# Key transposes evacuated in 1024-column tiles by one engine, and output products of 512 columns with a fold

## The chip, the cores and the metric

The kernel runs on one core of one Trainium2 chip. The time is device microseconds of one execution. Its engines are TensorE (PE, with its weight loads shown as PEld), VectorE (DVE), ScalarE (ACT), GpSimd (POOL) and SyncE (SP); 16 DMA engines move data between HBM and the on-chip memory SBUF. TensorE writes into PSUM, eight banks of 512 float32 columns in each of 128 partitions. Only DVE and ACT read PSUM here.

## The reference

One decoding step for two rows x of 512 numbers. Everything is float32.

```
xn  = layernorm(x)
q   = xn @ wq                                  # 32 heads of 128
k,v = the last 4096 positions of the caches    # 8 key/value heads, each serves 4 query heads
o   = softmax(q . k / sqrt(128)) @ v           # per head
A   = o @ wo                                   # 4096 -> 512
h   = relu(xn @ W_gate) * (xn @ W_up)          # 512 -> 1792
B   = h @ W_down                               # 1792 -> 512
out = x + A + B
```

The keys and values are 2 x 8 x 4096 x 128 numbers each, 67 MB together. The weights are another 28 MB.

## The kernel before

All large inputs go through one ring of four SBUF buffers (`ring`, 32 KB a partition each), in program order, by DMAs that SP issues. A load waits on SP until the buffer of the load four places ahead of it is released. The order is wq in two parts, W_gate, W_up, then key and value tiles of 4 MB, then W_down, then wo in two parts of 4 MB (the second cut into rows 0 to 7, 8 to 12, 13 to 14 and 15).

The attention is done in four groups g (batch row and half of the key/value heads), each with two key tiles and two value tiles (a = 0, 1; two heads each). The order of instructions is written out by hand: the tile framework is told to keep it and only adds the waits. Each engine runs its own instructions strictly in that order.

A key tile arrives as 64 blocks of 128 x 128 (positions by head dimension) and has to be transposed. `transposes` (L308 to L319) does it in two halves (s1 = 0, 1) of 32 blocks: four blocks go into one PSUM tile `pk` of 512 columns, and `evacuate` (L304 to L306) copies it to the SBUF tile `kT`, the copies taken in turn by ACT and DVE. `pk` has three buffers in the pool `ps_kt`, whose tag `kt` also serves `q_ps`, `qt`, `g_ps`, `u_ps`, `pp` and `y_ps`. `scores` (L322) multiplies a finished half of `kT` with the queries, 16 instructions of 512 columns in four column groups of 32. It runs one half behind the transposes.

`softmax(g - 1)` (L335) is a generator. Its steps are put between the transposes of key tile (g, 0), from the third PSUM tile on, by `kwork` (L432): the row maximum `m` and its transpose `mt` and combination `mx`, `mb` on DVE, the bias `nm` by a small matmul, the exponentials `p` on ACT, then two transposed halves `pp` in PSUM, which DVE multiplies with a mask into `pt`.

`values` (L386) multiplies `pt` with a value tile, 32 instructions of 512 columns in four column groups, and `evacuate` copies the sum `o` to `on`. `gather` (L404) picks each head's rows with four matmuls of 128 columns; `finish` (L414) scales by the softmax's sum. `spread_heads` (L420) brings the heads of two groups into the transposed form `oT` that the last product needs.

The last product: `project` (L478) adds one row block (128 inputs) to `y_ps`, as four matmuls of 128 columns in four column groups. It is called for the 17 blocks of W_down, then for the 2 x 16 blocks of wo, as their loads land. `y_ps` is copied to `yo` and stored.

Before the groups, the kernel computes xn, the queries, and the hidden layer `hh`, `hx`, whose transposes `ht_ps` (104 + 8 small matmuls) become `hT`.

Of the kernel before, what the change touches and what calls it, by code (L numbers as in the profile page):

```python
# [20 lines left out]
def kernel(  # L21
# [12 lines left out]
    nc = tc.nc  # L34
    P = 128
    B, _, D = x.shape
    _, HKV, SK, DH = k_cache.shape
# [86 lines left out]
    NJ = HQ * DH // (R * P)  # L124
    NE = DH // NJ
    HR = HQ // R
# [11 lines left out]
    ident = const.tile([P, P], F32, name="ident")  # L138
# [5 lines left out]
    ones = const.tile([1, 1], F32, name="ones")  # L144
# [6 lines left out]
    hx = const.tile([32, SX, 64], F32, name="hx")  # L151
# [19 lines left out]
    )  # L171


    HK = 2 * REP
    by_h = const.tile([P, NP, HK], F32, name="by_h")
    nc.vector.tensor_reduce(
# [66 lines left out]

    g_ps = ps_kt.tile([P, MQ], F32, name="g_ps", tag="kt")
    u_ps = ps_kt.tile([P, MQ], F32, name="u_ps", tag="kt")
    x_ps = ps_1.tile([32, 2, FX], F32, name="x_ps", tag="o0")
    for h, dst, wt in ((0, g_ps, gw), (1, u_ps, uw)):
        for kc in range(KC):
            for c in range(Q):
# [28 lines left out]
    for i in range(LEFT):  # L278
# [1 line left out]
        nc.vector.tensor_tensor(  # L280
            hx[:, RX, i:32:4], gx[:, 1, lo:lo + 8], x_ps[:, 1, lo:lo + 8], op=ALU.mult
        )
    ht_ps = ps_1.tile([P, FM + SX, B], F32, name="ht_ps", tag="misc")
    for k in range(FM):
        for c in range(Q):
            nc.tensor.matmul(
                ht_ps[32 * c:32 * c + 32, k], hh[:, k], ident[:, 32 * c:32 * c + B], start=True, stop=True
            )
    for k in range(SX):
        m = 64 if k < RX else 32  # L290
        nc.tensor.matmul(ht_ps[0:m, FM + k], hx[:, k, 0:m], ident[0:32, 0:B], start=True, stop=True)
    nc.vector.tensor_copy(hT[:, 0:FM, :, 0], ht_ps[:, 0:FM])
    nc.vector.tensor_copy(hT[0:64, FM:FM + RX, :, 0], ht_ps[0:64, FM:FM + RX])
    if LEFT:
        nc.vector.tensor_copy(hT[0:32, FM + RX, :, 0], ht_ps[0:32, FM + RX])

    HW = W // S1
    ss, pts, rls = {}, {}, {}  # L300
    kts, osb = {}, {}
    turn = [0]

    def evacuate(dst, src):  # L304
        (nc.vector.tensor_copy if turn[0] % 2 else nc.scalar.copy)(dst, src)  # L305
        turn[0] += 1  # L306

    def transposes(g, a, s1, kt_in):  # L308

        kt = ktp.tile([P, 2, HW], F32, name=f"kT{g}_{a}_{s1}", tag="kT")  # L310
        kts[g, a, s1] = kt
        for n in range(2 * Q):
            pk = ps_kt.tile([P, 512], F32, name=f"pk{g}_{a}_{s1}_{n}", tag="kt")
            for u in range(4):
                j = 8 * Q * s1 + 4 * n + u
                nc.tensor.transpose(pk[:, u * P:(u + 1) * P], kt_in[:, j * P:(j + 1) * P], ident)  # L316
# [18 lines left out]
    def softmax(g):  # L335

        m = work.tile([P, 1], F32, name=f"m{g}", tag="m")
        nc.vector.tensor_reduce(out=m, in_=ss[g], op=ALU.max, axis=AX.X)
# [8 lines left out]
        nc.vector.tensor_scalar(  # L347
            mb, mx[:, :, None, :].to_broadcast([1, NP, S1, HK]), -SCALE, None, op0=ALU.mult
        )
        yield  # L350
        nm_ps = ps_1.tile([P, 1], F32, name=f"nm_ps{g}", tag="misc")
        for q in range(Q):
            nc.tensor.matmul(
                nm_ps[32 * q:32 * q + 32, :], mb.rearrange("p a s k -> p (a s k)"), ones, start=True, stop=True
            )
# [12 lines left out]
        pv = p.rearrange("r y h -> r (y h)")  # L368
        for jh in range(2):
            pp = ps_kt.tile([P, 4, P], F32, name=f"pp{g}_{jh}", tag="kt")  # L370
            for u in range(4):
                lo = (4 * jh + u) * P
                nc.tensor.transpose(pp[:, u], pv[:, lo:lo + P], ident)  # L373
            nc.vector.tensor_tensor(  # L374
                pts[g][:, jh].rearrange("p n u k -> p u n k"), pp.rearrange("p u (n k) -> p u n k", k=HK),
                own.rearrange("p h i -> p (h i)")[:, None, None, :].to_broadcast([P, 4, Q * NP * S1, HK]), op=ALU.mult,
            )
# [6 lines left out]
    ons = {}  # L384

    def values(g, a, v):  # L386
        o = ps_1.tile([P, 512], F32, name=f"o{g}_{a}", tag=f"o{a}")
        for s1 in range(S1):
            for jh in range(2):
                for q in range(Q):  # L390
                    n = (q * NP + a) * S1 + s1
                    lo = (8 * Q * s1 + 8 * q + 4 * jh) * P
                    nc.tensor.matmul(  # L393
                        o[32 * q:32 * q + 32, :],
                        pts[g][:, jh, n].rearrange("p u k -> p (u k)"), v[:, lo:lo + 512],
                        start=(s1 == 0 and jh == 0), stop=(s1 == S1 - 1 and jh == 1),
                    )
# [6 lines left out]
    def gather(g, a):  # L404

        if a == 0:
            oa[g] = ps_1.tile([HR, P], F32, name=f"oa{g}", tag="oa")
        for u in range(4):
            nc.tensor.matmul(  # L409
                oa[g], pick[:, u, 8 - 8 * a:24 - 8 * a], ons[a][:, u],  # L410
                start=(a == 0 and u == 0), stop=(a == NP - 1 and u == 3),
            )

    def finish(g):  # L414
        r, b = divmod(g, B)
        if b == 0:
            osb[r] = const.tile([HR, B, P], F32, name=f"osb{r}")
        nc.vector.tensor_scalar(osb[r][:, b], oa[g], rls[g], 2.0, op0=ALU.mult, op1=ALU.mult)

    def spread_heads(r):  # L420
        op = ps_1.tile([P, NJ, B], F32, name=f"op{r}", tag="misc")
# [53 lines left out]
            x2[:, e * P:(e + 1) * P], start=True, stop=False,  # L475
        )

    def project(lhsT, w, stop):  # L478
        for e in range(Q):
            nc.tensor.matmul(  # L480
                y_ps[32 * e:32 * e + 17, :], lhsT.rearrange("p b s -> p (b s)")[:, 0:17],
                w[:, e * P:(e + 1) * P], start=False, stop=stop,
            )

    for a in range(NP):
# [1 line left out]
        gather(g, a)  # L487
    finish(g)
    for k in range(FM):
        project(hT[:, k], dw[:, k], False)  # L490
    for k in range(SX):
        n = 64 if k < RX else 32
        project(hT[0:n, FM + k], wx[0:n, k], False)
    spread_heads(R - 1)
    for r, cuts in ((0, (0, NJ)), (1, (0, 8, 13, 15, NJ))):
        wt = ring.tile([P, NJ, D], F32, name=f"wo{r}", tag="ring")
        for j0, j1 in zip(cuts, cuts[1:]):
# [34 lines left out]
```

## Time and profile before

| | |
|---|---|
| median of 3 runs | 231.21 us (231.04 to 231.34) |
| the profiled execution's own time | 231.43 us |
| its span, first to last instruction | 229.6 us |
| mean granted TensorE clock | 0.938 |
| moved by DMA | 95.15 MB, 414 GB/s on average |
| busy: PE, DVE, ACT | 81%, 29%, 20% of the span |

The span is what the trace covers; the profiled execution's own time has 1.8 us around it. In the rows shown below, a line is: kernel line, engine, operation, output <- inputs, shapes, then either the group's busy time and the mean nanoseconds of one, or (in the timeline) start and duration in microseconds, with the idle time before and what ended it in brackets. A float32 matmul is two PE instructions, a transpose one. Ends of matmuls are modelled, so starts are the safer numbers on PE.

### The profile page before, as it was taken

The page shows a single profiled execution, that of the slowest core. Times are in us where ns is not written, and L with a number is a line of the kernel's source. Part 1 is how long each engine was busy: PE and PEld are TensorE (multiplying, and loading weights), DVE is VectorE, ACT ScalarE, POOL GpSimd, SP SyncE. Part 2 cuts the span into 40 slices and gives each one's busy share as a digit, 9 for nine tenths or more (in the row PEclk, how much of TensorE's full clock was granted, in tenths as well). Part 3 has the DMA queues.
Part 4 walks back from the last instruction along what each step waited for, and adds up shares of the span by engine and source line. Part 5 has one row for each costly group of instructions (what it writes and reads, how often), then busy time and mean ns, then how long its engine had stood idle before and what let it go on. Part 6 is the DMA issues. An engine that isn't in the chain of part 4 may idle for free.

```text
span 229.6 us, 4149 instructions
## 1 busy us (share of the span) xinstructions
PE 185.4 (81%) x1876; PEld 114.7 (50%) x1876; DVE 67.2 (29%) x135; ACT 46.9 (20%) x80; POOL 8.2 (4%) x25
## 2 busy tenths in 40 slices
PE   0059961779999899997799699889979973988794
PEld 0052231259666583663484566458446532247682
DVE  0320021034444570441472143157124224001000
ACT  0020100004344451440351233045023202010000
POOL 8100000000000000000000000000000300000000
PEclk9999999577999999999999799999999999599678
DMA  7999999999999999999999999999999999999981
GB/s 274 451 428 408 454 410 437 422 451 442 405 425 451 415 417 445 442 411 420 457 417 432 428 440 414 434 445 414 422 440 437 417 428 440 423 442 414 410 364 49
DMA packets 3824, 95.15 MB, mean 414 GB/s; under 512 B 434, under 2 KB 448, under 8 KB 704
## 3 DMA queue, kind: packets, MB, share of 16 engines
q1 hardware_dynamic: 3796, 94.90, 96.7%
q8 instruction: 14, 0.23, 0.4%
q14 instruction: 2, 0.02, 0.0%
q10 hardware_dynamic: 12, 0.00, 0.0%
HBM read 94.90 MB, written 0.00 MB: 413 GB/s over the span
## 4 chain that ended last, share of the span: by engine, by line
DMA 54%; PE 41%; DVE 2%; issue 1%; ACT 1%; ACTq 0%; POOL 0%; DVEq 0%
DMA k<-in_A_k_cache_dram 37%; PE pk L316 21%; DMA wo<-in_A_wo_dram 13%; PE s L329 7%; PE y_ps L480 5%; DMA x<-in_A_x_dram 4%; PE o L393 3%; PE q_ps L222 3%; PE xt_ps L212 2%; ACT p L362 1%; PE pp L373 0%; ACTq L135 0%; PE oa L409 0%; DVE stats L189 0%; DVE kT L305 0%
## 5 line engine op out<-in xcount | busy, mean ns | idle before, releaser
L316 PE MATMUL pk<-ident,k 128*128 128x128 f32 x512 | 67.9, 286 | 6.0 <-DMA k<-in_A_k_cache_dram 5.9
L316 PEld LDWEIGHTS pk<-ident,k 128*128 128x128 f32 x512 | 57.9, 146 | 20.9 <-issue 16.7
L305 DVE COPY kT<-pk 128x512 f32<-128x512 f32 x64 | 44.2, 691 | 52.1 <-PE pk L316 46.2
L305 ACT COPY kT<-pk 128x512 f32<-128x512 f32 x64 | 37.5, 585 | 69.5 <-PE pk L316 69.5
L393 PE MATMUL o<-v,pt 128*32 128x512 f32 x256 | 32.5, 641 | 0.0
L329 PE MATMUL s<-kT,qz 128*32 128x512 f32 x256 | 30.9, 598 | 0.0
L393 PEld LDWEIGHTS o<-v,pt 128*32 128x32 f32 x256 | 11.3, 117 | 15.7 <-issue 10.9
L212 PE MATMUL xt_ps<-rep,xn 2*128 2x32 f32 x16 | 3.7, 400 | 13.9 <-DVE xn L206 13.9
L329 PEld LDWEIGHTS s<-kT,qz 128*32 128x32 f32 x256 | 7.1, 109 | 11.9 <-issue 11.5
L305 DVE COPY on<-o 128x512 f32<-128x512 f32 x4 | 2.8, 692 | 30.5 <-PE o L393 30.5
L409 PE MATMUL oa<-on,pick 128*16 128x128 f32 x64 | 8.3, 273 | 4.1 <-DVE on L305 3.3
L480 PE MATMUL y_ps<-wo,oT 128*17 128x128 f32 x256 | 10.3, 329 | 1.6 <-DMA wo<-in_A_wo_dram 1.6
L409 PEld LDWEIGHTS oa<-on,pick 128*16 128x16 f32 x64 | 5.8, 97 | 11.3 <-DVE on L305 7.0
L250 PE MATMUL u_ps<-wu,xnT 128*32 128x416 f32 x32 | 5.8, 901 | 6.1 <-DMA wu<-in_B_W_up_dram 6.1
L212 PEld LDWEIGHTS xt_ps<-rep,xn 2*128 2x128 f32 x16 | 3.6, 320 | 13.9 <-issue 13.9
L222 PE MATMUL q_ps<-wq,xnT 128*32 128x512 f32 x64 | 9.7, 777 | 0.5 <-DVE xnT L214 0.5
L480 PEld LDWEIGHTS y_ps<-wo,oT 128*17 128x17 f32 x256 | 8.1, 119 | 3.6 <-DMA wo<-in_A_wo_dram 2.6
L305 ACT COPY on<-o 128x512 f32<-128x512 f32 x4 | 2.3, 586 | 27.0 <-PE o L393 27.0
L98 POOL MEMSET wx<- 64x2048 f32 x1 | 1.8, 1804 | 169.1 <-PE s L329 169.1
L362 ACT ACTIVATE p<-s,nm 128x1024 f32<-128x1024 f32 x4 | 4.5, 1114 | 13.1 <-DVE nm L357 13.1
L374 DVE TENSOR_TENSOR pt<-pp,own 128x512 f32<-128x512 f32 x8 | 5.4, 689 | 2.6 <-PE pp L373 2.6
L373 PE MATMUL pp<-ident,p 128*128 128x128 f32 x32 | 4.9, 280 | 1.7 <-ACT p L362 1.5
(83 smaller groups left out, 68.2 us busy)
## 6 DMA issues: line engine op xcount, KB each, us to landing
k<-in_A_k_cache_dram SPq DMA_DIRECT2D x8, 4096.0 KB, 23.9
v<-in_A_v_cache_dram SPq DMA_DIRECT2D x8, 4096.0 KB, 28.3
wq<-in_A_wq_dram SPq DMA_DIRECT2D x2, 4096.0 KB, 21.7
wo<-in_A_wo_dram SPq DMA_DIRECT2D x1, 4096.0 KB
wg<-in_B_W_gate_dram SPq DMA_DIRECT2D x1, 3584.0 KB, 29.8
wu<-in_B_W_up_dram SPq DMA_DIRECT2D x1, 3584.0 KB, 39.3
wd<-in_B_W_down_dram SPq DMA_DIRECT2D x1, 3328.0 KB
wo<-in_A_wo_dram SPq DMA_DIRECT2D x1, 2048.0 KB
```

The lines of the kernel that those rows point to most:

```text
L212: nc.tensor.matmul(xt_ps[:, o, kc, :], cols, rep.rearrange("r s b -> r (s b)"), start=True, stop=True)
L222: nc.tensor.matmul(q_ps[r][32 * c:32 * c + 32, :], xnT[:, 0, kc, :], wqt[kc // 2][:, kc % 2, n * 512:(n + 1) * 512], start=(kc == 0), stop ...
L250: nc.tensor.matmul(dst[32 * c:32 * c + 32, :], xnT[:, 1, kc, :], wt[:, kc, c * MQ:(c + 1) * MQ], start=(kc == 0), stop=(kc == KC - 1),)
L305: (nc.vector.tensor_copy if turn[0] % 2 else nc.scalar.copy)(dst, src)
L316: nc.tensor.transpose(pk[:, u * P:(u + 1) * P], kt_in[:, j * P:(j + 1) * P], ident)
L329: nc.tensor.matmul(ss[g][32 * q:32 * q + 32, :], qz[:, g, 32 * n:32 * n + 32], kt[:, h, q * 512:(q + 1) * 512], start=(a == 0 and s1 == 0 ...
L362: nc.scalar.activation(p, both, AF.Exp, bias=nm, scale=SCALE, accum_out=l)
L373: nc.tensor.transpose(pp[:, u], pv[:, lo:lo + P], ident)
L374: nc.vector.tensor_tensor(pts[g][:, jh].rearrange("p n u k -> p u n k"), pp.rearrange("p u (n k) -> p u n k", k=HK), own.rearrange("p h i ...
L393: nc.tensor.matmul(o[32 * q:32 * q + 32, :], pts[g][:, jh, n].rearrange("p u k -> p (u k)"), v[:, lo:lo + 512], start=(s1 == 0 and jh == 0 ...
L409: nc.tensor.matmul(oa[g], pick[:, u, 8 - 8 * a:24 - 8 * a], ons[a][:, u], start=(a == 0 and u == 0), stop=(a == NP - 1 and u == 3),)
L480: nc.tensor.matmul(y_ps[32 * e:32 * e + 17, :], lhsT.rearrange("p b s -> p (b s)")[:, 0:17], w[:, e * P:(e + 1) * P], start=False, stop=stop,)
```

## The change

The transposes of a half go into four PSUM tiles of 1024 columns (two banks), eight blocks each, with two buffers instead of three; DVE copies all of them, ACT none. The generator still yields eight times a half: after four blocks and after the copy. `o` has one buffer instead of two. `on` is no longer a copy but a product with a row mask on DVE; `gather` is then one matmul of 512 columns, and `finish` adds up its four parts with one DVE reduction. `mb` is written four times wide by two DVE instructions, and `nm` comes from one matmul instead of four. `ht_ps` is made by 13 + 4 matmuls with a strided identity, and copied by five DVE copies. Three constants are added.

In the last product, `slot` multiplies one row block by all 512 columns in one matmul; four blocks in turn use the four column groups of a second PSUM tile `y4`. That serves W_down, the first half of wo and rows 0 to 7 of the second half. Then DVE copies `y4` to `ys`, four matmuls with the constant `fold` add its column groups into `y_ps`, and the last eight rows of wo go on as before, in quarters.

```diff
-    ps_kt = ctx.enter_context(tc.tile_pool(name="ps_kt", bufs=3, space=PSUM))
+    ps_kt = ctx.enter_context(tc.tile_pool(name="ps_kt", bufs=2, space=PSUM))
...
+    mask = const.tile([P, 4], F32, name="mask")
+    nc.vector.tensor_reduce(out=mask, in_=pick[:, :, 8:16], op=ALU.add, axis=AX.X)
+    picks = const.tile([P, 24], F32, name="picks")
+    nc.vector.tensor_reduce(out=picks, in_=pick.rearrange("p u c -> p c u"), op=ALU.add, axis=AX.X)
+    fold = const.tile([P, 32], F32, name="fold")
+    nc.vector.tensor_reduce(
+        out=fold, in_=ident.rearrange("p (t c) -> p c t", t=Q), op=ALU.add, axis=AX.X
+    )
...
-    ht_ps = ps_1.tile([P, FM + SX, B], F32, name="ht_ps", tag="misc")
+    ht_ps = ps_1.tile([64, FM * Q + SX, B], F32, name="ht_ps", tag="misc")
+    firsts = ident.rearrange("p (c r) -> p c r", c=Q)[:, :, 0:B]
     for k in range(FM):
-        for c in range(Q):
-            nc.tensor.matmul(
-                ht_ps[32 * c:32 * c + 32, k], hh[:, k], ident[:, 32 * c:32 * c + B], start=True, stop=True
-            )
+        nc.tensor.matmul(ht_ps[0:32, k * Q:(k + 1) * Q], hh[:, k], firsts, start=True, stop=True)
...
-        for n in range(2 * Q):
-            pk = ps_kt.tile([P, 512], F32, name=f"pk{g}_{a}_{s1}_{n}", tag="kt")
-            for u in range(4):
-                j = 8 * Q * s1 + 4 * n + u
+        for n in range(Q):
+            pk = ps_kt.tile([P, 1024], F32, name=f"pk{g}_{a}_{s1}_{n}", tag="kt")
+            for u in range(8):
+                j = 8 * Q * s1 + 8 * n + u
                 nc.tensor.transpose(pk[:, u * P:(u + 1) * P], kt_in[:, j * P:(j + 1) * P], ident)
-            evacuate(
-                kt[:, :, n * 256:(n + 1) * 256], pk.rearrange("p (y h) -> p h y", h=2),
+                if u == 3:
+                    yield
+            nc.vector.tensor_copy(
+                kt[:, :, n * 512:(n + 1) * 512], pk.rearrange("p (y h) -> p h y", h=2)
             )
             yield
...
-        mb = work.tile([1, NP, S1, HK], F32, name=f"mb{g}", tag="mb")
-        nc.vector.tensor_scalar(
-            mb, mx[:, :, None, :].to_broadcast([1, NP, S1, HK]), -SCALE, None, op0=ALU.mult
-        )
+        mb = work.tile([1, Q, NP, S1, HK], F32, name=f"mb{g}", tag="mb")
+        for s1 in range(S1):
+            nc.vector.tensor_scalar(
+                mb[:, :, :, s1], mx[:, None].to_broadcast([1, Q, NP, HK]), -SCALE, None, op0=ALU.mult
+            )
...
-        o = ps_1.tile([P, 512], F32, name=f"o{g}_{a}", tag=f"o{a}")
+        o = ps_1.tile([P, 512], F32, name=f"o{g}_{a}", tag="o")
...
-        evacuate(ons[a].rearrange("p u d -> p (u d)"), o)
+        nc.vector.tensor_tensor(
+            ons[a], o.rearrange("p (u d) -> p u d", u=4), mask[:, :, None].to_broadcast([P, 4, P]), op=ALU.mult
+        )
...
-            oa[g] = ps_1.tile([HR, P], F32, name=f"oa{g}", tag="oa")
-        for u in range(4):
-            nc.tensor.matmul(
-                oa[g], pick[:, u, 8 - 8 * a:24 - 8 * a], ons[a][:, u],
-                start=(a == 0 and u == 0), stop=(a == NP - 1 and u == 3),
-            )
+            oa[g] = ps_1.tile([HR, 4, P], F32, name=f"oa{g}", tag="oa")
+        nc.tensor.matmul(
+            oa[g], picks[:, 8 - 8 * a:24 - 8 * a], ons[a], start=(a == 0), stop=(a == NP - 1)
+        )
...
-        nc.vector.tensor_scalar(osb[r][:, b], oa[g], rls[g], 2.0, op0=ALU.mult, op1=ALU.mult)
+        su = work.tile([HR, P], F32, name=f"su{g}", tag="su", bufs=1)
+        nc.vector.tensor_reduce(out=su, in_=oa[g].rearrange("h u d -> h d u"), op=ALU.add, axis=AX.X)
+        nc.vector.tensor_scalar(osb[r][:, b], su, rls[g], 2.0, op0=ALU.mult, op1=ALU.mult)
...
+    y4 = ps_kt.tile([P, D], F32, name="y4", tag="kt")
+    cuts = {0: (0, NJ), 1: (0, 8, 13, 15, NJ)}
+    EARLY = FM + SX + NJ + cuts[1][1]
+    done = [0]
+
+    def slot(lhsT, w):
+        t, i = done[0] % Q, done[0]
+        nc.tensor.matmul(
+            y4[32 * t:32 * t + 32, :], lhsT.rearrange("p b s -> p (b s)"), w, start=(i < Q), stop=(i >= EARLY - Q)
+        )
+        done[0] += 1
...
         for j in range(NJ):
-            project(oT[:, r, j], wt[:, j], (r, j) == (R - 1, NJ - 1))
+            if (r, j) < (1, cuts[1][1]):
+                slot(oT[:, r, j], wt[:, j])
+                continue
+            if j == cuts[1][1]:
+                ys = work.tile([P, D], F32, name="ys", tag="qs")
+                nc.vector.tensor_copy(ys, y4)
+                quarters(fold[:, 0:17], ys, False)
+            quarters(oT[:, r, j].rearrange("p b s -> p (b s)")[:, 0:17], wt[:, j], (r, j) == (R - 1, NJ - 1))
```

More of the change, by code (lines that the diff above doesn't have):

```diff
@@ L245 @@
     u_ps = ps_kt.tile([P, MQ], F32, name="u_ps", tag="kt")
-    x_ps = ps_1.tile([32, 2, FX], F32, name="x_ps", tag="o0")
+    x_ps = ps_1.tile([32, 2, FX], F32, name="x_ps", tag="o")
     for h, dst, wt in ((0, g_ps, gw), (1, u_ps, uw)):
@@ L282 @@
         )
-    ht_ps = ps_1.tile([P, FM + SX, B], F32, name="ht_ps", tag="misc")
+    ht_ps = ps_1.tile([64, FM * Q + SX, B], F32, name="ht_ps", tag="misc")
+    firsts = ident.rearrange("p (c r) -> p c r", c=Q)[:, :, 0:B]
     for k in range(FM):
-        for c in range(Q):
-            nc.tensor.matmul(
-                ht_ps[32 * c:32 * c + 32, k], hh[:, k], ident[:, 32 * c:32 * c + B], start=True, stop=True
-            )
+        nc.tensor.matmul(ht_ps[0:32, k * Q:(k + 1) * Q], hh[:, k], firsts, start=True, stop=True)
     for k in range(SX):
[L290 to L295, printed above, removed]
+        nc.tensor.matmul(ht_ps[:, FM * Q + k], hx[:, k], ident[0:32, 0:B], start=True, stop=True)
+    for c in range(Q):
+        nc.vector.tensor_copy(hT[32 * c:32 * c + 32, 0:FM, :, 0], ht_ps[0:32, c:FM * Q:Q])
+    nc.vector.tensor_copy(hT[0:64, FM:, :, 0], ht_ps[:, FM * Q:])
     HW = W // S1
@@ L301 @@
     kts, osb = {}, {}
[L302 to L306, printed above, removed]
     def transposes(g, a, s1, kt_in):
@@ L345, in softmax @@
         )
-        mb = work.tile([1, NP, S1, HK], F32, name=f"mb{g}", tag="mb")
-        nc.vector.tensor_scalar(
-            mb, mx[:, :, None, :].to_broadcast([1, NP, S1, HK]), -SCALE, None, op0=ALU.mult
-        )
+        mb = work.tile([1, Q, NP, S1, HK], F32, name=f"mb{g}", tag="mb")
[3 more added lines that the diff above has]
+            )
         yield
         nm_ps = ps_1.tile([P, 1], F32, name=f"nm_ps{g}", tag="misc")
-        for q in range(Q):
-            nc.tensor.matmul(
-                nm_ps[32 * q:32 * q + 32, :], mb.rearrange("p a s k -> p (a s k)"), ones, start=True, stop=True
-            )
+        nc.tensor.matmul(nm_ps, mb.rearrange("p q a s k -> p (q a s k)"), ones, start=True, stop=True)
         nm = work.tile([P, 1], F32, name=f"nm{g}", tag="nm")
@@ L476, with quarters @@
         )
-    def project(lhsT, w, stop):
+    y4 = ps_kt.tile([P, D], F32, name="y4", tag="kt")
[8 more added lines that the diff above has]
+        done[0] += 1
+    def quarters(lhsT, w, stop):
         for e in range(Q):
             nc.tensor.matmul(
-                y_ps[32 * e:32 * e + 17, :], lhsT.rearrange("p b s -> p (b s)")[:, 0:17],
-                w[:, e * P:(e + 1) * P], start=False, stop=stop,
+                y_ps[32 * e:32 * e + 17, :], lhsT, w[:, e * P:(e + 1) * P], start=False, stop=stop
             )
@@ L489 @@
     for k in range(FM):
-        project(hT[:, k], dw[:, k], False)
+        slot(hT[:, k], dw[:, k])
     for k in range(SX):
-        n = 64 if k < RX else 32
-        project(hT[0:n, FM + k], wx[0:n, k], False)
+        slot(hT[0:64, FM + k], wx[0:64, k])
     spread_heads(R - 1)
-    for r, cuts in ((0, (0, NJ)), (1, (0, 8, 13, 15, NJ))):
+    for r in range(R):
         wt = ring.tile([P, NJ, D], F32, name=f"wo{r}", tag="ring")
-        for j0, j1 in zip(cuts, cuts[1:]):
+        for j0, j1 in zip(cuts[r], cuts[r][1:]):
             nc.sync.dma_start(wt[:, j0:j1], wo_rows(r, j0, j1))
         for j in range(NJ):
-            project(oT[:, r, j], wt[:, j], (r, j) == (R - 1, NJ - 1))
+            if (r, j) < (1, cuts[1][1]):
[6 more added lines that the diff above has]
+            quarters(oT[:, r, j].rearrange("p b s -> p (b s)")[:, 0:17], wt[:, j], (r, j) == (R - 1, NJ - 1))
     yo = work.tile([P, P], F32, name="yo", tag="yo", bufs=1)
```

2 lines of the change are left out of this document (removed).

## The prediction

> **What bounds the kernel now.** I read the page's header, its slices and its chain first, then the chain in order of time, the waits, the timeline of the key tiles, and the timeline of the end.
>
> ```profile
> span 229.6 us, 4149 instructions
> ...
> PE 185.4 (81%) x1876; PEld 114.7 (50%) x1876; DVE 67.2 (29%) x135; ACT 46.9 (20%) x80; POOL 8.2 (4%) x25
> ...
> DMA  7999999999999999999999999999999999999981
> ...
> DMA 54%; PE 41%; DVE 2%; issue 1%; ACT 1%; ACTq 0%; POOL 0%; DVEq 0%
> ```
>
> The DMA engines are busy in every slice from the second to the last but one, and the chain alternates between DMA and PE: one stream of loads sets the time, and PE follows close behind.
>
> ```profile
> 51.36 8.97 PE pk L316 x64
> ...
> 87.49 3.43 PE o L393 x32
> ...
> 100.73 28.26 DMA k<-in_A_k_cache_dram
> ...
> 140.45 28.97 DMA k<-in_A_k_cache_dram
> ...
> 216.27 7.96 PE y_ps L480 x189
> ...
> 224.27 1.29 PE y_ps L480 x40
> ...
> 225.55 0.63 PE y_ps L480 x16
> ...
> 226.20 0.46 PE y_ps L480 x8
> ```
>
> The second key tile of group 2 lands at 100.73 + 28.26 = 128.99 us, that of group 3 at 169.42. Four 4 MB tiles lie between, so a tile takes 10.1 us. At the end PE is caught by the landings of wo's last pieces (224.27, 225.55, 226.20), so here the transfers bound it to the last matmul at 226.66. How far PE is from being the bound shows in what it waits for:
>
> ```profile
> PE pk L316 <- DMA k<-in_A_k_cache_dram: 5.9, 4, 2.1
> ```
>
> From 51 us to 186 us PE waits 5.9 us for keys in all. That is its whole reserve.
>
> **The change part by part.** The evacuation first. Before, two engines take turns with 512 columns each and three PSUM tiles are in rotation; afterwards DVE alone copies 1024 columns, with two tiles.
>
> ```profile
> L305 DVE COPY kT<-pk 128x512 f32<-128x512 f32 x64 | 44.2, 691 | 52.1 <-PE pk L316 46.2 <-ACT on L305 5.2
> L305 ACT COPY kT<-pk 128x512 f32<-128x512 f32 x64 | 37.5, 585 | 69.5 <-PE pk L316 69.5
> ...
> L214 DVE COPY xnT<-xt_ps 128x256 f32<-128x256 f32 x1 | 0.4, 423 | 3.9 <-PE xt_ps L212 3.9
> ```
>
> No 1024-column DVE copy is in the trace. From 256 to 512 columns it grows by (691 - 423)/256 = 1.05 ns a column, so 691 + 512 x 1.05 = 1.23 us. The ends are 1.14 (the pitch below) and 2 x 0.691 = 1.38; I take 1.23, the straight line through the two rows.
>
> ```profile
> 62.11 3.92 PE L316 MATMUL pk<-ident,k 128*128 128x128 f32 x32
> ...
> 63.30 0.69 DVE L305 COPY kT<-pk 128x512 f32<-128x512 f32 x1 [2.24 <-PE pk L316]
> ...
> 65.96 1.92 PE L329 MATMUL s<-kT,qz 128*32 128x512 f32 x16
> ...
> 67.82 3.92 PE L316 MATMUL pk<-ident,k 128*128 128x128 f32 x32
> ...
> 119.21 0.69 DVE L374 TENSOR_TENSOR pt<-pp,own 128x512 f32<-128x512 f32 x1 [0.20 <-PE pp L373]
> ...
> 119.81 0.68 DVE L305 COPY kT<-pk 128x512 f32<-128x512 f32 x1
> ...
> 185.59 0.69 DVE L305 COPY on<-o 128x512 f32<-128x512 f32 x1 [6.04 <-PE o L393]
> ...
> 186.34 0.94 PE L409 MATMUL oa<-on,pick 128*16 128x128 f32 x7 [0.83 <-DVE on L305]
> ```
>
> A half tile (32 transposes, then 16 score matmuls) takes PE 67.82 - 62.11 = 5.71: 0.965 for eight transposes (T) four times, 1.85 for scores. A DVE copy starts 63.30 - 62.11 = 1.19 after the first of its eight transposes. Back-to-back DVE work overlaps by 0.09 (119.81 after 119.21, each 0.69), so copies (C) can follow at 1.14. PE goes on 0.06 after the copy it waits for (185.59 + 0.69 to 186.34).
>
> A plain half, from 0: C1 1.19 to 2.42; T2 ends 1.93, C2 2.33 to 3.55. T3 needs C1's buffer and starts at 2.48, C3 3.67 to 4.89. T4 needs C2's: 3.61 to 4.58. Scores to 6.42, during which DVE catches up. 6.42 against 5.71: **+0.71 a half, +1.4 a tile**.
>
> The first tile of a group carries the softmax of the group before; DVE does both, and `pp` shares the two buffers.
>
> ```profile
> 109.68 1.06 PE L316 MATMUL pk<-ident,k 128*128 128x128 f32 x8 [0.96 <-DMA k<-in_A_k_cache_dram]
> ...
> 112.67 0.69 DVE L338 TENSOR_REDUCE m<-s 128x1 f32<-128x512 f32 x1 [1.14 <-PE s L329]
> ...
> 114.58 0.17 DVE L347 TENSOR_SCALAR mb<-mx 1x32 f32<-1x32 f32 x1
> ...
> 114.89 0.24 PE L353 MATMUL nm_ps<-ones,mb 1*32 1x1 f32 x8 [0.72 <-DVE mb L347]
> ...
> 121.69 1.92 PE L329 MATMUL s<-kT,qz 128*32 128x512 f32 x16
> ```
>
> Before, 121.69 - 109.68 = 12.0 to the last scores. Afterwards, from 0: T1, scores to 2.8, T2 to 3.8; DVE does `m` (at 2.96, as 112.67 is 2.99 after the start before) and C2 (4.0 to 5.2) before `mx` and `mb`, so `nm_ps` waits until 5.84 (1.5 instead of 0.72), with all transposes queued behind it. T3 then ends 6.4, T4 7.35; C3 ends 7.8, C4 8.97. `pp` of the first half needs C3's buffer (7.9), T5 needs C4's (9.03). T6 stops half-way at 10.5, because the second `pp` needs T5's copy (11.45); its masking ends 12.9, C6 14.0. T7 starts at 12.96 or 14.1, as it gets `pp`'s buffer or C6's, and the last scores at 15.1 or 16.0. I take 15.5 between two cases I can't tell apart: **+3.5**.
>
> The Trainium skill, page "TensorEngine Tiling (Array Packing)", section "PSUM Bottleneck", advises both ScalarE and VectorE for evacuation, and access vectorized over several tiles. The change follows the second and drops the first; by the rows ACT and DVE together finish 1024 columns in 0.69, against 1.23, and the sum above is the sum by the first half of the rule.
>
> The first tile (group 0) starts at the half clock, which hides part: its eighth T ends about 1.8 later than at 60.3 (four copies paced at 1.24, half of 1.19 + 1.23 + 0.06, where T takes 0.965, and 0.7 before). Sum of lag to the last values of group 2: 1.8 + 1.4 + 3 x (3.5 + 1.4) = 17.9.
>
> ```profile
> 129.12 5.48 PE L316 MATMUL pk<-ident,k 128*128 128x128 f32 x32 [2.07 <-DMA k<-in_A_k_cache_dram]
> ...
> 169.55 0.63 PE L316 MATMUL pk<-ident,k 128*128 128x128 f32 x4 [1.57 <-DMA k<-in_A_k_cache_dram]
> ```
>
> Against it stand the waits that vanish, 0.96 + 2.07 + 1.57, and the slow clock after the 2.07 (5.48 instead of 3.92), 6.1 in all. **Lag 11.8 us.**
>
> The ring frees late by the same, and SP, which waits there in order, issues late:
>
> ```profile
> k<-in_A_k_cache_dram SPq DMA_DIRECT2D x8, 4096.0 KB, 23.9
> ```
>
> A key load lands 23.9 us after its issue (median), one tile takes 10.1, so about 14 are in hand and the queue stays fed. Tightest are wo's last four loads: they wait for the first values of group 3, 195.47 + 6.37 + 11.8 = 213.6 below, and the load ahead of them has landed by 216.27; 2.6 us are left, and their rows are wanted only from 229.5.
>
> The end, a chain on PE alone:
>
> ```profile
> 195.47 6.37 PE L393 MATMUL o<-v,pt 128*32 128x512 f32 x32
> ...
> 208.72 3.09 PE L480 MATMUL y_ps<-wd,hT 128*17 128x128 f32 x101
> ...
> 212.74 1.97 PE L423 MATMUL op<-osb,spread 16*128 16x32 f32 x16
> ...
> 216.27 10.35 PE L480 MATMUL y_ps<-wo,oT 128*17 128x128 f32 x256 [1.57 <-DMA wo<-in_A_wo_dram]
> ```
>
> From 195.47 to 214.71 nothing in it waits for a load, so all of it shifts by 11.8. A slot (512 columns, four column groups) is the form of the values: 16 took 3.43 (32 instructions in the chain, at 87.49), 0.214 each. 17 slots for w_down take 3.6 instead of 4.0 (208.72 to 212.74): -0.4. The mask multiply, by the `pt` row, costs 0.69 as the copy did. `spread` ends at 214.7 + 11.8 - 0.4 = 226.1. Then nothing waits for a load (wo was complete at 226.2): 24 slots 5.1 to 231.3, drain, copy of `y4` (0.69) and hand-offs 1.0, fold 0.3, and the eight rows left in quarters 2.1 (1.29 + 0.63 + 0.46 less 0.3 of waits): 234.7, against 226.66. **+8.0.**
>
> Costed at nothing, each with its cover and its price without it:
>
> ```profile
> 10.60 0.68 DVE L189 BATCH_NORM_STATS2 stats<-x 2x6 f32<-2x512 f32 x1 [2.93 <-DMA x<-in_A_x_dram]
> ```
>
> the three set-up reductions (DVE idles 2.93 before `stats`; else 0.9, all on the path); the shorter `ht` and five `hT` copies (they come before the first keys at 51.36; uncovered, 0.5); the gather's 2 long matmuls for 8 short (0.67 either way, at most +0.2 each, 1.4 in all); the sum over `u` in `finish` (0.69 like `m`, beside 1.19 of transposes, at the end beside 3.6 of slots; uncovered 0.7 a group); `o` in one buffer (its first reader is done before the next values start; uncovered 0.7).
>
> The sum goes against the profiled execution, 231.43 (span 229.6 and 1.8 around it), 0.2 above the median 231.21: 231.2 + 8.0 = **239.2**.
>
> **The rivals.** *The copies stay hidden (not slower).* DVE would be busy 67.2 - 44.2 + 64 x 1.23 = 102 us, 45%: harmless as a share. If stalls came to under about 8 us in all, the 6.1 of reserve and the 1.57 before wo would swallow them, the last piece would still land at 226.2, and the time be 231.2, or a shade less. Two buffers and 1.23 against 0.965 speak against: 8 us would be under half of my sum.
>
> *Only the end suffers.* No lag, but slots at the half clock (6.37 for 16) finish 24 rows at about 224.3, as before, and copy and fold (1.3) then stand in the path of the last eight: +0.7 to +1.2, 232.1.
>
> *The clock.* PE's stalls let the clock fall.
>
> ```profile
> 126.00:129.40 3.40, 1.33 (x15) 0.44 (x8) 0.00 (x0) 0.58 (x1) 0.00 (x0) 0.99 1.09 463
> 166.90:170.30 3.40, 1.83 (x19) 0.91 (x12) 0.03 (x1) 0.58 (x1) 0.00 (x0) 1.00 0.94 405
> ...
> 129.40:132.80 3.40, 3.40 (x19) 3.40 (x18) 1.38 (x2) 0.77 (x2) 0.00 (x0) 0.51 0.92 395
> ```
>
> 3.4 us with 1.33 of PE were followed by 0.51, 3.4 us with 1.83 weren't. The softmax tile has 3.4 us near that (10.5 to 13.9: 1.1 to 2.0 busy). Each fall costs some 1.7 (3.4 us at half), three such tiles and the narrow `spread` 6.8: 246. The Trainium skill, "TensorE: Matmul & The Clock Gate", Part 4, says that transposes don't count as PE-busy; by that every tile would fall, but here the clock went from 0.51 back to 1.00 after 3.4 us of transposes alone, so the trace disagrees.
>
> **How the numbers follow.** My forecast 0.72, the clock 0.14, the end alone 0.08, hidden 0.06 (of which 0.02 below). Within 0.2% is what a measurement of this kernel can't tell from no change. Low end: 0.5 a half and +2.5 for softmax give a lag of 6.7 and +2.9, 234. High end: 16.0 in the softmax tile (+1.5), the long gathers (+1.4) and one fall of the clock (1.7): 244.
>
> **What would show it.** Right: `kT` copies of 1.2 us on DVE, PE's transposes waiting for them some 0.3 to 0.5 each, the key waits gone after group 0, a second key tile of group 3 begun about 10 us late, and after 226 us a PE chain with no DMA in it. Wrong: waits for keys that remain; a last wo piece that lands after 228 (the lag over the time in hand); or clock rows of 0.5 between 60 and 190 us.

## The result, and the profile after

The changed kernel takes 238.78 us (median of 6 runs, 237.42 to 239.29) against 231.32 us before (6 runs): 1.031 times as long, 95% interval 1.0288 to 1.0332. The profiled execution took 238.96 us, with a span of 237.2. The forecast was 239.2.

The page of the changed kernel, header, slices and chain:

```profile
span 237.2 us, 3310 instructions
...
PE 185.2 (78%) x1488; PEld 100.5 (42%) x1488; DVE 106.7 (45%) x154; ACT 7.4 (3%) x12; POOL 8.2 (3%) x25
...
PEclk9999979788999999999999999999999999569999
DMA  7999999999999999999999999999999999999800
...
PE 61%; DVE 19%; DMA 15%; issue 2%; ACT 0%; ACTq 0%; POOL 0%; DVEq 0%
```

The roles have changed. DMA, busy almost to the end before, is now done two slices (12 us) ahead of it, and its share of the chain falls from 54% to 15%; PE and DVE now hold 80% of the chain. PE's busy time is the same 185 us with 388 fewer matmul instructions: it works no longer, it stands still more. The chain in order of time leaves DMA at the first keys and never comes back:

```profile
22.87 27.98 DMA k<-in_A_k_cache_dram
...
124.96 1.11 PE pk L314 x8
126.09 1.24 DVE kT L317
...
127.37 0.67 PE pp L371 x4
128.07 0.69 DVE pt L372
128.76 1.13 DVE kT L317
...
206.15 6.43 PE o L391 x32
...
224.11 1.90 PE op L423 x16
226.01 5.33 PE y L485 x48
231.36 0.70 DVE ys L515
232.11 2.20 PE y_ps L492 x72
```

PE and DVE hand the work to and fro, one tile at a time, and after 190 us a chain of PE alone follows. What PE waits for (total, times, longest):

```profile
PE pk L314 <- DVE kT L317: 5.3, 14, 0.4
PE nm_ps L353 <- DVE mb L348: 4.9, 4, 1.4
...
PE pp L371 <- DVE kT L317: 4.3, 6, 0.9
...
PE pk L314 <- DMA k<-in_A_k_cache_dram: 2.4, 1, 2.4
```

Of the four waits for keys only the first is left; instead there are some 15 us of waits for DVE (2.8 of them, for `mb`, stood before too). The timeline of one softmax tile and of the two plain halves behind it:

```profile
115.70 1.09 PE L314 MATMUL pk<-ident,k 128*128 128x128 f32 x8
...
121.58 0.35 PE L353 MATMUL nm_ps<-ones,mb 1*128 1x1 f32 x2 [1.37 <-DVE mb L348]
...
127.37 0.66 PE L371 MATMUL pp<-ident,p 128*128 128x128 f32 x4 [0.88 <-DVE kT L317]
...
128.81 2.22 PE L314 MATMUL pk<-ident,k 128*128 128x128 f32 x16 [0.21 <-DVE pt L372]
130.97 1.93 PE L329 MATMUL s<-kT,qz 128*32 128x512 f32 x16
...
136.25 1.97 PE L314 MATMUL pk<-ident,k 128*128 128x128 f32 x16
138.67 2.23 PE L314 MATMUL pk<-ident,k 128*128 128x128 f32 x16 [0.44 <-DVE kT L317]
140.82 1.93 PE L329 MATMUL s<-kT,qz 128*32 128x512 f32 x16
142.68 1.97 PE L314 MATMUL pk<-ident,k 128*128 128x128 f32 x16
```

A half takes 142.68 - 136.25 = 6.43 us, a softmax tile 130.97 - 115.70 = 15.27 to its last scores. DVE's large copies, from the page, and the mask multiply behind the last values of group 2, from the timeline:

```profile
L317 DVE COPY kT<-pk 128x1024 f32<-128x1024 f32 x64 | 76.1, 1221 | 18.8 <-PE pk L314 18.2
...
195.09 0.69 DVE L397 TENSOR_TENSOR on<-o,mask 128x512 f32<-128x512 f32 x1 [4.95 <-PE o L391]
```

The last values of group 2 end at 195.09, where the multiply starts, instead of 185.59: PE is 9.5 us late.

### The profile page after: what moved, and what is told of

Read it like the earlier page. It is cut to its first block, busy times and chain, and to the rows that moved or that the text cites. A ratio compares the mean times of both kernels' runs of the same rounds, so it can differ in the third digit from the quotient of the medians.

```text
span 237.2 us, 3310 instructions
## 1 busy us (share of the span) xinstructions
PE 185.2 (78%) x1488; PEld 100.5 (42%) x1488; DVE 106.7 (45%) x154; ACT 7.4 (3%) x12; POOL 8.2 (3%) x25
## 4 chain that ended last, share of the span: by engine, by line
PE 61%; DVE 19%; DMA 15%; issue 2%; ACT 0%; ACTq 0%; POOL 0%; DVEq 0%
PE pk L314 19%; DVE kT L317 14%; PE o L391 13%; PE s L329 12%; DMA k<-in_A_k_cache_dram 12%; PE y L485 4%; DMA x<-in_A_x_dram 4%; PE oa L408 3%; PE q_ps L230 2%; PE pp L371 2%; PE op L423 2%; PE xt_ps L220 2%; DVE on L397 1%; DVE pt L372 1%; PE y_ps L492 1%
## 5 line engine op out<-in xcount | busy, mean ns | idle before, releaser
L317 DVE COPY kT<-pk 128x1024 f32<-128x1024 f32 x64 | 76.1, 1221 | 18.8 <-PE pk L314 18.2
L391 PE MATMUL o<-v,pt 128*32 128x512 f32 x256 | 35.0, 642 | 0.0
L397 DVE TENSOR_TENSOR on<-o,mask 128x512 f32<-128x512 f32 x8 | 5.5, 692 | 38.2 <-PE o L391 38.2
L391 PEld LDWEIGHTS o<-v,pt 128*32 128x32 f32 x256 | 9.3, 117 | 20.1 <-issue 20.0
L408 PE MATMUL oa<-on,picks 128*16 128x512 f32 x16 | 8.2, 596 | 4.2 <-DVE on L397 4.2
L258 PE MATMUL u_ps<-wu,xnT 128*32 128x416 f32 x32 | 4.6, 736 | 4.6 <-DMA wu<-in_B_W_up_dram 4.6
L371 PEld LDWEIGHTS pp<-ident,p 128*128 128x128 f32 x32 | 4.1, 161 | 7.3 <-ACT p L360 3.9
L258 PE MATMUL g_ps<-wg,xnT 128*32 128x416 f32 x32 | 4.4, 716 | 2.5 <-DMA wg<-in_B_W_gate_dram 2.5
L408 PEld LDWEIGHTS oa<-on,picks 128*16 128x16 f32 x16 | 1.1, 95 | 10.8 <-DVE on L397 8.9
L485 PE MATMUL y<-wo,oT 128*32 128x512 f32 x48 | 5.4, 594 | 0.0
## 6 DMA issues: line engine op xcount, KB each, us to landing
k<-in_A_k_cache_dram SPq DMA_DIRECT2D x8, 4096.0 KB, 17.8
```

The costliest lines, as they stand in the source:

```text
L258: nc.tensor.matmul(dst[32 * c:32 * c + 32, :], xnT[:, 1, kc, :], wt[:, kc, c * MQ:(c + 1) * MQ], start=(kc == 0), stop=(kc == KC - 1),)
L317: nc.vector.tensor_copy(kt[:, :, n * 512:(n + 1) * 512], pk.rearrange("p (y h) -> p h y", h=2))
L391: nc.tensor.matmul(o[32 * q:32 * q + 32, :], pts[g][:, jh, n].rearrange("p u k -> p (u k)"), v[:, lo:lo + 512], start=(s1 == 0 and jh == 0 ...
L397: nc.vector.tensor_tensor(ons[a], o.rearrange("p (u d) -> p u d", u=4), mask[:, :, None].to_broadcast([P, 4, P]), op=ALU.mult)
L408: nc.tensor.matmul(oa[g], picks[:, 8 - 8 * a:24 - 8 * a], ons[a], start=(a == 0), stop=(a == NP - 1))
L485: nc.tensor.matmul(y4[32 * t:32 * t + 32, :], lhsT.rearrange("p b s -> p (b s)"), w, start=(i < Q), stop=(i >= EARLY - Q))
```

## The experiments

What was open: whether it is the engine (DVE alone has too much to copy) or the buffers (two large tiles let PE run only one tile ahead) that makes the stalls; whether the rest of the change, above all the new end, has a part in the loss; and whether the waits for keys are a reserve that an early delay can use up for nothing.

**Two engines, large tiles.** ACT and DVE copy in turn:

```diff
-            nc.vector.tensor_copy(
+            (nc.vector.tensor_copy if n % 2 else nc.scalar.copy)(
                 kt[:, :, n * 512:(n + 1) * 512], pk.rearrange("p (y h) -> p h y", h=2)
             )
```

> The changed kernel, but ACT and DVE copy the 1024-column tiles in turn; still two buffers. Theory (the two-buffer loop: transposes 0.965 + hand-off 0.22 + copy + 0.06 before a buffer can be filled again): an ACT copy of 1024 columns takes about 1.03 us (585 ns at 512, 254 at 128), so a half tile still takes about 6.25 instead of 6.42, a softmax tile about 14.9 instead of 15.3; the lag shrinks by some 2.5 us only: about 236.3 us. Rival (one engine can't keep up with the copies): with two engines the lag is gone, 231.5 to 232.5 us.

Measured: 235.56 us, ratio 1.0174 (1.0156 to 1.0192). Three of the timeline's PE rows, and the groups of its copies by DVE and ACT:

```profile
95.73 1.97 PE L314 MATMUL pk<-ident,k 128*128 128x128 f32 x16
97.97 2.19 PE L314 MATMUL pk<-ident,k 128*128 128x128 f32 x16 [0.27 <-ACT kT L317]
...
101.95 1.97 PE L314 MATMUL pk<-ident,k 128*128 128x128 f32 x16
```

```profile
L317 DVE COPY kT<-pk 128x1024 f32<-128x1024 f32 x32 | 39.1, 1223 | 42.5 <-PE pk L314 41.8 <-PE mt L341 0.7
...
L317 ACT COPY kT<-pk 128x1024 f32<-128x1024 f32 x32 | 32.4, 1012 | 90.2 <-PE pk L314 81.1 <-DVE osb L418 9.1
```

With half the copies taken off DVE, PE still stalls at the third tile, now for ACT: a half takes 101.95 - 95.73 = 6.22, where the buffer theory had 6.25. DVE idles over 40 us before its copies. The total is 0.7 us below the 236.3 expected, and 3 us above the rival's 232.5. A second engine bought back less than half of the loss, and in the half no more than ACT's shorter copy (1.01 us against 1.22) explains.

**One engine, small tiles.** DVE alone copies, but 512 columns into four buffers, the same PSUM:

```diff
-    ps_kt = ctx.enter_context(tc.tile_pool(name="ps_kt", bufs=2, space=PSUM))
+    ps_kt = ctx.enter_context(tc.tile_pool(name="ps_kt", bufs=4, space=PSUM))
...
-        for n in range(Q):
-            pk = ps_kt.tile([P, 1024], F32, name=f"pk{g}_{a}_{s1}_{n}", tag="kt")
-            for u in range(8):
-                j = 8 * Q * s1 + 8 * n + u
+        for n in range(2 * Q):
+            pk = ps_kt.tile([P, 512], F32, name=f"pk{g}_{a}_{s1}_{n}", tag="kt")
+            for u in range(4):
+                j = 8 * Q * s1 + 4 * n + u
                 nc.tensor.transpose(pk[:, u * P:(u + 1) * P], kt_in[:, j * P:(j + 1) * P], ident)
-                if u == 3:
-                    yield
             nc.vector.tensor_copy(
-                kt[:, :, n * 512:(n + 1) * 512], pk.rearrange("p (y h) -> p h y", h=2)
+                kt[:, :, n * 256:(n + 1) * 256], pk.rearrange("p (y h) -> p h y", h=2)
             )
```

> The changed kernel, but DVE alone copies 512-column tiles, with four buffers (the same four PSUM banks). Theory (two-buffer loop): eight copies at a pitch of 0.60 are 4.8 us in a half tile of 5.71, and four buffers let PE run ahead, so plain halves stall no more; a softmax tile has 12.4 us of DVE work in 12.0 and costs 1 to 1.5 more; in all less than the 6.1 us that PE has to spare, so about 231.8 us. Rival (one engine can't keep up): DVE has more to do than with large copies (4.8 against 4.6 a half), so it is as slow as the changed kernel or slower, 238 to 240 us.

Measured: 232.51 us, ratio 1.0046 (1.0032 to 1.0061), 0.7 us above the theory and far below the rival. PE and DVE in its timeline:

```profile
91.79 3.93 PE L314 MATMUL pk<-ident,k 128*128 128x128 f32 x32
95.65 1.92 PE L327 MATMUL s<-kT,qz 128*32 128x512 f32 x16
97.50 3.89 PE L314 MATMUL pk<-ident,k 128*128 128x128 f32 x32
```

```profile
92.53 4.86 DVE L315 COPY kT<-pk 128x512 f32<-128x512 f32 x8
```

The same engine copies the same columns, in twice as many instructions (4.86 us a half instead of 4.77), and PE doesn't stall at all: 97.50 - 91.79 = 5.71, the half of the kernel before. The softmax tile takes 13.2 (from 109.31 to 122.50 in the same timeline) and not 12.0: there DVE's queue still tells, by 1.2. Between the first two runs the theory is decided: what stalls PE in the plain halves is the buffers, their size and number. With small tiles, copying with one engine costs something only in the softmax tile. Size and number were changed together here, in the same PSUM, so the two are not told apart.

**Both engines, small tiles.** The same, with the copies in turn on ACT and DVE:

```diff
-            nc.vector.tensor_copy(
+            (nc.vector.tensor_copy if n % 2 else nc.scalar.copy)(
                 kt[:, :, n * 256:(n + 1) * 256], pk.rearrange("p (y h) -> p h y", h=2)
             )
```

> The changed kernel, but ACT and DVE copy 512-column tiles in turn, with four buffers: everything of the change but the evacuation. Theory: no lag, so what is left is the end of the kernel: 231.2 us if the transfers still end last there, up to 232.2 if the copy of y4 and the fold stand in the path. Rival (the products of 512 columns and the gathers cost or save by themselves): more than 232.5, or under 230.5 us.

Measured: 231.60 us, ratio 1.0015 (1.0003 to 1.0027). PE's waits:

```profile
PE pk L314 <- DMA k<-in_A_k_cache_dram: 7.9, 4, 2.6
...
PE y L483 <- DMA wo<-in_A_wo_dram: 3.4, 1, 3.4
```

All four waits for keys are back, and larger than before (5.9). Everything of the change but the evacuation costs at most 0.3%.

**The old end on the changed kernel.** `slot`, `y4` and `fold` replaced by the product in quarters:

```diff
-    for k in range(FM):
-        slot(hT[:, k], dw[:, k])
-    for k in range(SX):
-        slot(hT[0:64, FM + k], wx[0:64, k])
+    for k in range(FM):
+        project(hT[:, k], dw[:, k], False)
+    for k in range(SX):
+        n = 64 if k < RX else 32
+        project(hT[0:n, FM + k], wx[0:n, k], False)
...
-            if (r, j) < (1, cuts[1][1]):
-                slot(oT[:, r, j], wt[:, j])
-                continue
...
+            project(oT[:, r, j], wt[:, j], (r, j) == (R - 1, NJ - 1))
```

> The changed kernel, with the last product as before (quarters into y_ps, no y4, no fold). Theory: the lag of 9.5 us stays; saved are the drain, the copy of y4 and the fold (1.1 us), given back are 0.4 us of the W_down products: about 238.0 us. Rival (the end of the kernel is where most was lost): 235 us or less.

Measured: 237.02 us, ratio 1.0235 (1.0212 to 1.0257). Its end in the timeline:

```profile
219.08 3.00 PE L480 MATMUL y_ps<-wd,hT 128*17 128x128 f32 x98
222.01 1.07 PE L480 MATMUL y_ps<-wx,hT 64*17 64x128 f32 x32
223.01 1.97 PE L423 MATMUL op<-osb,spread 16*128 16x32 f32 x16
224.91 7.63 PE L480 MATMUL y_ps<-wo,oT 128*17 128x128 f32 x256
```

With PE late, the end with slots is the slower one. W_down takes 3.9 us here (219.08 to 223.01), with slots 4.9 (219.12 to 224.04), where I had expected slots to save 0.4. wo takes 7.6 here, and 8.4 (225.94 to 234.31) with slots, copy and fold, though a single slot (5.36 us for 24) is no slower than a block in quarters (7.63 for 32). The gain of 1.8 us is twice what I had expected, and still a quarter of the loss.

**The copies alone.** The kernel before, with the transposes of the change:

```diff
-    ps_kt = ctx.enter_context(tc.tile_pool(name="ps_kt", bufs=3, space=PSUM))
+    ps_kt = ctx.enter_context(tc.tile_pool(name="ps_kt", bufs=2, space=PSUM))
...
-        for n in range(2 * Q):
-            pk = ps_kt.tile([P, 512], F32, name=f"pk{g}_{a}_{s1}_{n}", tag="kt")
+        for n in range(Q):
+            pk = ps_kt.tile([P, 1024], F32, name=f"pk{g}_{a}_{s1}_{n}", tag="kt")
...
-        o = ps_1.tile([P, 512], F32, name=f"o{g}_{a}", tag=f"o{a}")
+        o = ps_1.tile([P, 512], F32, name=f"o{g}_{a}", tag="o")
```

> The kernel before, with only the transposes as in the change (1024 columns, two buffers, DVE alone) and one buffer for o; gathers, products, copies of o as before. Theory: nearly all of the loss comes with it: the same lag of 9 to 10 us, without copy and fold at the end: 237 to 238 us. Rival (the loss is spread over the parts): 234 us or less.

Measured: 237.31 us, ratio 1.0249 (1.0192 to 1.0305): some four fifths of the loss (0.025 of 0.031; by the interval, between three fifths and all of it), with nothing else changed but the one buffer for `o`.

**Half the groups, first attempt.** Large DVE copies in two of the four groups. In the other two, ACT was to copy the first half of a large tile while PE filled its second:

```diff
                 if u == 3:
+                    if not g < 2:
+                        nc.scalar.copy(
+                            kt[:, :, n * 512:n * 512 + 256], pk[:, 0:512].rearrange("p (y h) -> p h y", h=2)
+                        )
                     yield
...
+                nc.vector.tensor_copy(
+                    kt[:, :, n * 512 + 256:(n + 1) * 512], pk[:, 512:1024].rearrange("p (y h) -> p h y", h=2)
+                )
```

> The changed kernel, with the large DVE copies in groups 0 and 1 alone; in groups 2 and 3 ACT copies the first half of each tile as soon as it is there, and DVE the second, so that no buffer is late. Theory (a reserve of 6.1 us between 109 and 170 us): the lag of 7.3 us at the end of group 1 is eaten up by the waits for keys in groups 2 and 3 and the wait for wo: 231.5 to 232.5 us. Rival (every large copy costs the same, wherever it stands): half of the loss, 235 us.

> The same the other way round: large DVE copies in groups 2 and 3 alone. Theory: 3.2 + 1.4 in group 2, of which the wait before the second key tile and the slow clock after it eat 3.6, then 3.2 + 1.4 in group 3 less 1.6: a lag of 3.0 to 4.0 at the last values of group 2, and copy and fold behind it: 233.5 to 235 us, above the version with the early groups by 2 us. Rival (every large copy costs the same): the two versions equal, 235 us.

Measured: 259.03 us (ratio 1.1204, 1.1172 to 1.1235) and 265.15 us (1.1488, 1.1415 to 1.1561). Both theories missed, because the repair did not do what I meant. The timeline of the second:

```profile
51.86 0.59 ACT L317 COPY kT<-pk 128x512 f32<-128x512 f32 x1 [5.20 <-PE pk L314]
...
52.49 1.97 PE L314 MATMUL pk<-ident,k 128*128 128x128 f32 x8 [0.68 <-ACT kT L317]
...
55.14 1.97 PE L314 MATMUL pk<-ident,k 128*128 128x128 f32 x8 [0.68 <-ACT kT L317]
```

PE waits 0.68 for the ACT copy of the first bank before it writes the second: the waits that the framework puts in are those of the whole tile, and eight transposes take 55.14 - 52.49 = 2.65 us. That is at the half clock (granted 0.50 from 52 to 68 us); at the full clock, from 76 us on, the wait is the same 0.68 and eight transposes take 1.78 (76.44 to 78.22 in the same run). Two banks in one tile are one buffer, not two. Whether the chip would need that wait was not tried. For the question of the reserve these two runs say nothing.

**Half the groups, with two PSUM pools.** The large tiles (two buffers) in groups 0 and 1 alone, then a second pool with four buffers of 512 columns, copied in turn by ACT and DVE:

```diff
+    first = ExitStack()
+    ps_kt = first.enter_context(tc.tile_pool(name="ps_ka", bufs=2, space=PSUM))
...
     for g in range(1, NG):
+        if g == 2:
+            first.close()
+            ps_kt = ctx.enter_context(tc.tile_pool(name="ps_kb", bufs=4, space=PSUM))
```

> The changed kernel; the large DVE copies with two buffers in groups 0 and 1 alone, small tiles of 512 columns with four buffers, copied by ACT and DVE in turn, in groups 2 and 3 (two PSUM pools, one after the other). Theory (PE has a reserve of about 6 us in its waits for keys between 109 and 170 us): PE is 7 us late at the end of group 1, but the waits of groups 2 and 3 eat that up; the last scores start at about 187, as in the kernel before: 231.5 to 232.5 us. Rival (every large copy costs the same, wherever it stands): half of the loss, 235 us.

Measured: 231.29 us, ratio 1.0003 (0.9989 to 1.0017). And the other way round, four small buffers first, two large ones from group 2 on (bufs=4, then bufs=2):

> The same the other way round: large DVE copies in groups 2 and 3 alone. Theory: groups 0 and 1 end with time to spare, which is lost as a wait for keys at 109 us; from there the large copies cost 2 x (3.2 + 1.4) us, less the wait before the second key tile of group 2 and the clock after it; last scores at about 190.8, 5 us before the changed kernel's: 233.7 us, some 2 us above the version with the early groups. Rival (every large copy costs the same): both versions equal, 235 us.

Measured: 233.03 us, ratio 1.0054 (1.0025 to 1.0082). PE's timeline at the borders, first with the early groups stalled, then with the late ones (one fence for each):

```profile
107.65 1.92 PE L341 MATMUL s<-kT,qz 128*32 128x512 f32 x16
...
185.60 0.64 PE L341 MATMUL s<-kT,qz 128*32 128x512 f32 x3
```

```profile
98.93 1.92 PE L341 MATMUL s<-kT,qz 128*32 128x512 f32 x16
...
109.27 1.65 PE L316 MATMUL pk<-ident,k 128*128 128x128 f32 x8 [2.27 <-DMA k<-in_A_k_cache_dram]
...
191.01 0.64 PE L341 MATMUL s<-kT,qz 128*32 128x512 f32 x3
```

And the version with small tiles throughout, which has the same end and no stalls:

```profile
99.08 1.92 PE L327 MATMUL s<-kT,qz 128*32 128x512 f32 x16
...
183.85 0.64 PE L327 MATMUL s<-kT,qz 128*32 128x512 f32 x3
```

With the early groups stalled PE is as late at the end of group 1 as in the changed kernel (107.65, and 107.70 in the changed kernel, against 100.63 before), and at the last scores of all it is not late any more (185.60, against 187.01 before and 195.85 in the changed kernel). The same stalls in groups 2 and 3 find nothing behind them to eat them up, and the time that the quick groups 0 and 1 gained is lost waiting 2.27 us for keys at 109; the last scores come at 191.0. Part of the catching up is owed to the four small buffers in groups 2 and 3, which run a little faster than the kernel before (PE's waits for keys were 7.9 us with them in all groups, 5.9 before). Against small tiles throughout, PE with the early groups stalled is 8.6 us late at the end of group 1 and 1.75 at the last scores (185.60 - 183.85), so 6.8 us were eaten on the way; the rest fits into the 3.4 us that PE waited for wo there. With the late groups stalled it is 7.2 us late at the last scores. A stall costs by where it stands: the ratios of the two versions, 1.0003 and 1.0054, have intervals that don't touch.

**Small tiles and quarters.** Four small buffers on two engines, as above, with the old end as above; the rest of the change stays:

```diff
-            nc.vector.tensor_copy(
-                kt[:, :, n * 512:(n + 1) * 512], pk.rearrange("p (y h) -> p h y", h=2)
+            (nc.vector.tensor_copy if n % 2 else nc.scalar.copy)(
+                kt[:, :, n * 256:(n + 1) * 256], pk.rearrange("p (y h) -> p h y", h=2)
             )
...
-        slot(hT[:, k], dw[:, k])
+        project(hT[:, k], dw[:, k], False)
```

> The changed kernel with 512-column tiles, four buffers, ACT and DVE in turn, and the last product in quarters as before: what is left of the change is the masked gathers, the sum in finish, the shorter bias and hidden transposes. Theory: the transfers end it, as before: 231.2 to 231.5 us, at or up to 0.4 us below the same with y4 and fold. Rival (the end costs nothing; what the small version lacks against the kernel before lies elsewhere): 231.6 us or more, as with y4 and fold.

Measured: 231.32 us, ratio 0.9997 (0.9988 to 1.0005). Against the same with `y4` and fold (1.0015, 1.0003 to 1.0027) the end costs some 0.2%, with intervals that just touch. The rest of the change (masked gathers, `finish`, bias, hidden transposes) neither costs nor saves anything that could be measured. No version beat the kernel before: where PE is early, the transfers end it at the same time.

## Why the prediction was right

The forecast was +8.0 us, slower, by a lag of PE that the end can't hide; measured against the runs before it is +7.5 (238.78 - 231.32), in the profiled executions +7.5 too (238.96 - 231.43). The mechanism is the one forecast: two large buffers make PE wait for DVE, the waits for keys take back part of it, and a chain on PE shows the rest. That the total came within 0.5 us is partly luck, as the lag and the end were each off by about 2 us, in opposite directions. By its own steps:

- *The copy*, 1.23 us by the straight line: 1.221 (mean of 64).
- *A plain half*, +0.71: 6.43 against 5.71, +0.72. The wait stands where it was put: PE at the third tile, 0.44 us.
- *The softmax tile*, 15.1 or 16.0, taken as 15.5: 15.27. `nm_ps` waits 1.37 (1.5 forecast), the second `pp` 0.88 for T5's copy (1.0 forecast), and T7 waits for `pt`, not for a copy: it got `pp`'s buffer, the first of the two cases.
- *The first tile*, +1.8: 61.47 - 50.99 = 10.5 to the first scores against 60.26 - 51.36 = 8.9, +1.6.
- *The reserve*, 6.1 us: the waits for keys but the first are gone, and the runs with half of the groups show the reserve at work.
- *The lag*, 11.8: 9.5. This term was mis-sized. The parts as measured give 1.6 + 1.4 + 3 x (3.3 + 1.4) - 6.1 = 11.0 and 0.4 less, as the first keys came 0.37 earlier. Half of what is then still over lies in the base: I took every half of the kernel before at 5.71, the row of group 0, but in groups 1 to 3 a half took 5.82 from scores to scores (134.53 to 140.35), so there the loss was 0.6 a half and not 0.71.
- *The end*, a chain on PE after 195: as forecast, with no DMA in it. Its terms were off in both directions. The lag grew from 9.5 to 10.6 before the first values of group 3 (206.08 against 195.47), mostly because `pp` ran at the half clock there (1.97 for eight transposes at a granted clock of 0.50, 1.09 at 1.00 before). W_down's 17 slots took 4.9 us (219.12 to 224.04), not 3.6. Of the 13 blocks of 128 rows one is left over after three rounds of four, and the first column group begins late, behind the gather: from 221.24 on, the last four instructions start one at a time, 0.43 apart, where four had started together, and the four blocks of 64 rows start only behind them, at 223.05. Copy, fold and the last eight rows took 3.0 (231.34 to 234.31), not 3.4. So the lag was 2.3 too large in the sum and the end behind it about 2 too small, and the errors cancelled: PE ends 7.65 us later (234.31 against 226.66).
- *The queue*: a key load landed 17.8 us after its issue instead of 23.9, still above the 10.1 that a tile takes. The DMA stayed fed; wo's last piece landed 12.4 us after its issue, before PE asked for it.

The rivals: the copies did not stay hidden. *Only the end suffers* is what the version with small tiles and `y4` (231.60) shows: in its profiled execution the 24 slots of wo ran from 216.18 to 224.18, to where the rival had them end (224.3), and copy and fold behind them moved PE's end to 227.16, 0.5 us later than before. So that mechanism exists, but at 0.2% in the medians and not at 0.7 to 1.2 us. *The clock* did not fall: between 60 and 190 us it stayed at 1.00, in spite of the stalls (one stretch of the changed kernel: length, busy times, then granted clock, DMA share and GB/s).

```profile
60.00:190.00 130.00, 113.96 (x918) 66.97 (x920) 82.46 (x93) 3.62 (x6) 0.00 (x0) 1.00 1.00 429
```

Nor did it fall behind the narrow `spread`: from 225 to 235 us it was 1.00, where the kernel before, from 216 to 222, had 0.54. The fall around the softmax of group 3 both kernels have: over the first values of that group it is 0.56 in each.

The Trainium skill's rule in "TensorE: Matmul & The Clock Gate", Part 4, that the full clock doesn't engage for transposes, which don't count as PE-busy the same way, is not borne out here either: in these 130 us stand stretches of nothing but transposes (136.25 to 140.82, with a wait of 0.44), and the clock stayed full.

The Trainium skill's advice in "TensorEngine Tiling (Array Packing)", section "PSUM Bottleneck", to use ScalarE and VectorE both, agrees with these runs at either tile size: 235.6 against 238.8 with large tiles, 231.6 against 232.5 with small ones. The buffers weigh more: one engine with four small buffers (232.5) beat two engines with two large ones (235.6). The prediction read the section's other advice too widely: the Trainium skill speaks there of vectorized access to tiles in the same bank, and a copy of 1024 columns takes in two banks, so the change does not follow it.

What the prediction put together, "DVE alone, with two tiles", the experiments took apart: its working went by the buffers (T3 needs C1's buffer), and it was mostly the buffers. Four small ones gave back 6.3 of the 7.5 us on DVE alone, a second engine 3.2 with large tiles and 0.9 with small ones.

## What to carry to other kernels

Before a PSUM tile is made larger to save on the fixed cost of copies, work out the loop of one buffer: fill, hand-off, copy, hand-off. Divided by the number of buffers it has to stay below the fill time; with two tiles of two banks it was 2.47/2 = 1.24 us against 0.965, with four tiles of one bank it is by the same sum (0.48 + 0.22 + 0.69 + 0.06)/4 = 0.36 against 0.48, on the same PSUM and the same engine. The copying engine's own pace has to fit only into the whole half: 4.86 us of copies in 5.71. And price a stall by what lies behind it: with small tiles in the other half, the stalls of the first half of this kernel cost nothing, as waits for loads followed, and those of the second 0.5%.

## What was not expected of the hardware

Kernels that end with a PE chain scattered more from run to run than those that end with the transfers: 237.42 to 239.29 for the changed kernel (6 runs), 235.29 to 238.64 with the copies alone (4), 231.34 to 233.91 with the late groups stalled (9), against 231.19 to 231.73 for the kernel before in 27 runs and 231.18 to 231.66 in 11 for the last variant. A part of it may be where the clock's falls and rises come: the first values of group 3, the same 32 instructions, took 6.43 us in the changed kernel and 5.10 in the last variant (granted clock 0.56 and 0.70 over them), after nearly the same pauses for the softmax. But the kernel before, which hardly scattered, took 6.37 in its profiled execution. How much of the scatter that explains was not tested.
